# Computing the first four FFN column tiles during the initial weight load, and keeping w_down resident

## The chip, the cores and the metric

The kernel runs on one core of a Trainium2 chip. The metric is the device time of one execution in microseconds; before the change it is 2283.39 us, the median of 13 runs (2270.49 to 2290.09).

## What is computed

Two branches over the same x (2048 tokens of 1024, bf16) are mixed token by token with a sigmoid gate. Branch A walks over 64 segments of 32 tokens, strictly one after the other, since each hands eight memory rows to the next. Branch B is a gated feed-forward net (FFN) with 3584 inner columns, and needs nothing of branch A. Cut to what matters:

```
g = sigmoid((x * gate_w).sum(-1, keepdims=True))
for s in range(64):                              # branch A
    h = concat(mem, x[32*s : 32*s+32])           # 8 + 32 rows of 1024
    q, k, v = h @ Wq, h @ Wk, h @ Wv             # 32 heads of 128
    p = softmax(mask(q @ k.T / sqrt(128)))
    o = (p @ v) @ Wo
    mem, a[s] = o[:8], o[8:]
b = (gelu_tanh(x @ w_gate) * (x @ w_up)) @ w_down   # branch B
out = g * a + (1 - g) * b
```

## The kernel before

The kernel is one list of operations (`op`), each put on one of five engines: TensorE (pe), ScalarE (act), VectorE (dve), GpSimd (pool) and SyncE (sp, which only issues DMAs). Each engine works through its own part of the list in the order written. `_Prog` derives the waits from the byte ranges and PSUM banks that each operation reads and writes; for a PSUM bank it waits for the last operation of every other engine on that bank, reader or writer. An operation that waits holds up everything written behind it on its engine. A DMA named with a lane also waits for the previous DMA of that lane to have landed.

Three stages follow one another.

**The prologue** (lines 465 to 492). x comes in 16 tiles of 128 tokens through eight buffers `px`. `do_x(T)` transposes a tile on TensorE into PSUM bank 6 or 7 (line 426). ScalarE copies half of it into `xq` (L433), VectorE the other half (L434), and VectorE copies the last eight tokens of each segment into `xr` (L435). ScalarE's queue then issues the writes of both to the scratch tensors `xq_scr` (L437) and `xr_scr` (L440). For the gate, GpSimd multiplies the tile by gate_w into the single buffer `gp` (L442), and VectorE sums it into a column of `dl` (L444). So GpSimd's next product waits for VectorE's sum. Between these, SyncE's queue loads the attention weights in pieces of 512 KB into SBUF slots `sl` (L364).

Each of Wk, Wq, Wv and Wo has 16 pieces, 64 in all, for 52 slots. Twelve slots (`PAIRS`) are shared by two pieces each, so that they are loaded again in every segment: `spent` issues the next load when a piece has been used. `first` issues the first load of a slot. The buffers of the prologue lie in the 13 slots of Wo, so that these are first loaded within segment 0, at its second step (line 803).

**The attention** (lines 772 to 901). Every segment is a list of 64 products (`proj`; L678 for k, q and v, L690 for o) in the order k0 q0 v0 k1 q1 o0 v1 o1, where 0 and 1 are halves of the heads. Between them stand scores, softmax and the product with v. The last eight tokens of four segments at a time are projected as "fills" (L705). They are evacuated (L578), some are transposed (L590), and the results go to scratch through two buffers `stage` and GpSimd's queue (L751, lane `fq`; L746). Segment 0 does ten such fills itself (`fill0`).

**The FFN** (lines 948 to 1027). Tokens go in four blocks of 512 (`fb`). For each block, a loop over the 28 column tiles `j` does two groups of eight 128x512 matmuls, gate and up (L958), into one of two pairs of banks. The gelu follows in five operations: Square (ScalarE, L968), a VectorE product (L969), Tanh (ScalarE, L972), and two VectorE products (L973, L976), the last of which writes `GT[:, j]`. Then two passes over w_down (L1017, and L999 at the very end) make the output of the block, and `mix` combines it with branch A. w_gate and w_up stay in SBUF once loaded, in five chunks of `CH` = 2, 5, 7, 7, 7 column tiles. w_down streams through three 1 MB buffers `wd` (L549), 49 loads, and is loaded whole into `wl` for the last pass (L992). x comes back from `xq_scr` (L530). `early` lists the FFN loads that are issued within the last segment. `last_tail` finishes branch A after the seventh column tile of block 0 and then issues the rest of the first loads.

Of the kernel before, what the change touches and what calls it, by code (L numbers as in the profile page):

```python
# [195 lines left out]
def bass_gated_mix__memory_aug_recurrent_mem_tr__geglu_ffn__prompt_kernel(  # L196
# [19 lines left out]
    SEG = 32  # L216
# [14 lines left out]
    with ExitStack() as es:  # L231
# [14 lines left out]
        a_scr = nc.dram_tensor("a_scr", [NSEG, SEG, D], BF16)  # L246

# [74 lines left out]
        for m in "kqvo":  # L322
            for i in range(8):
                if i in PAIRS[m]:
                    hosts.append([(m, 0, i), (m, 1, i)])
                else:
                    hosts += [[(m, 0, i)], [(m, 1, i)]]
# [68 lines left out]
        cur[0] = slots[home["o", 0, 0]].off  # L396
        NPX = min(NT, 8)
# [4 lines left out]
        xq = [al(f"xq{i}", [128, 4, KC, SEG]) for i in range(2)]  # L402
        xr = [al(f"xr{i}", [128, KC, 4, NB]) for i in range(2)]
        hR1 = al("hR1", [128, KC, 32])
        dl = al("dl", [128, NT], FP32)
        assert cur[0] <= top
        memT = al("memT", [128, 64], at=oRc.off)
        hT = hTs[0]

# [9 lines left out]
        def do_x(T):  # L419
            t = px[T % NPX]  # L420
            b = 6 + T % 2
            x2 = T % 2

            def f(e):
                for kc in range(KC):
                    ins = e.transpose(PBV[b][:, kc * 128:(kc + 1) * 128], t[:, kc * 128:(kc + 1) * 128], ident[:, :])
                return ins
            op("pe", f, rd=[t.r(), ident.r()], wr=[BK(b)])
            pv = PBV[b].rearrange("p (k i c) -> p i k c", k=KC, i=4)
            h = (hR, hR1)[T] if T < 2 else None  # L430
            to = h[:, :, :].rearrange("p k (i c) -> p k i c", i=4) if h else xr[x2][:, :, :, :]
            to_r = h.r() if h else xr[x2].r()
            op("act", lambda e: e.activation(xq[x2][:, 0:2, :, :], pv[:, 0:2], ACTF.Copy), rd=[BK(b)], wr=[xq[x2].r(0, 512)])  # L433
            op("dve", lambda e: e.tensor_copy(xq[x2][:, 2:4, :, :], pv[:, 2:4]), rd=[BK(b)], wr=[xq[x2].r(512, 1024)])  # L434
            op("dve", lambda e: e.tensor_copy(to, PBV[b].rearrange("p (k i c) -> p k i c", k=KC, i=4)[:, :, :, NR:SEG]),  # L435
               rd=[BK(b)], wr=[to_r])
            op("act", lambda e: e.dma_start(xq_scr[T, :, :, :], xq[x2][:, :, :, :].rearrange("p i k c -> p i (k c)")),  # L437
               rd=[xq[x2].r()], wr=[("D", "xq", T)], lane=f"xw{x2}")
            if T > 0:
                op("act", lambda e: e.dma_start(xr_scr[T], to.rearrange("p k i c -> p (k i c)")),  # L440
                   rd=[to_r], wr=[("D", "xr", T)], lane=f"xv{x2}")
            op("pool", lambda e: e.tensor_tensor(out=gp[:, :], in0=t[:, :], in1=gwb[:, :], op=ALU.mult),  # L442
               rd=[t.r(), gwb.r()], wr=[gp.r()])
            op("dve", lambda e: e.tensor_reduce(dl[:, T:T + 1], gp[:, :], AX.X, ALU.add), rd=[gp.r()], wr=[dl.r(T, T + 1)])  # L444

# [23 lines left out]
        load_x(1)  # L469
        load_x(2)  # L470
        for n, p in enumerate(range(16)):
            first(at_step(p, 0))
            if n + 3 < NPX:
                load_x(n + 3)
        op("pe", tr_mem, rd=[pm.r(), ident.r()], wr=[BK(5)])
        op("dve", lambda e: e.tensor_copy(memT[:, :], PBV[5][:, 0:64]), rd=[BK(5)], wr=[memT.r()])
        for T in range(NT):
            do_x(T)
            load_x(T + NPX)
            if T == 0:  # L480
                load_h(0)
                op("dve", lambda e: e.tensor_copy(hT[:, :, NR:32], memT[:, :].rearrange("p (k c) -> p k c", k=KC)),
                   rd=[memT.r()], wr=[hT.r()])
        for p in range(16, 24):
            first(at_step(p, 0))
        for mr in (("k", 1), ("q", 1), ("v", 1)):
            for i in range(8):
                first((*mr, i))
# [3 lines left out]
        op("dve", lambda e: e.reciprocal(gal[:, :], dl[:, :]), rd=[dl.r()], wr=[gal.r()])  # L492


        cur[0] = res0
        FB = min(S, 512)
        NFB = S // FB
        TB = FB // 128
        NPS = (TB + 1) // 2
        xT = al("xT", [128, TB, 4, KC, SEG])  # L500
        WD = 4
        wd = [al(f"wd{i}", [128, WD, D]) for i in range(3)]
        GT = al("GT", [128, NJ, FB])
        CH = (2, 5, 7, 7, 7)
        assert sum(CH) == NJ
        jch = [(c, jj) for c, n in enumerate(CH) for jj in range(n)]
        wg, wu = [], []
        for c, n in enumerate(CH):
            wg.append(al(f"wg{c}", [128, KC, n * 128]))
            wu.append(al(f"wu{c}", [128, KC, n * 128]))  # L510
        assert cur[0] <= top
        free = [(low, res0), (cur[0], top)]
# [8 lines left out]
        tp = [al2(f"tp{t}", [128, FB], FP32) for t in range(2)]  # L521
        s1 = al2("s1", [128, FB], FP32)
        assert s1.off < res0
# [10 lines left out]
        def load_w(c):  # L534
            c0, c1 = sum(CH[:c]) * 128, sum(CH[:c + 1]) * 128
# [4 lines left out]
        NWD = NJ // WD  # L540
        nwd = [0]

        def load_wd():
            n = nwd[0]
            nwd[0] += 1
            if n >= (NFB * NPS - 1) * NWD:
                return
            c = n % NWD
            op("sp", lambda e: e.dma_start(wd[n % 3][:, :, :],  # L549
                                           B_w_down[c * WD * 128:(c + 1) * WD * 128, :].rearrange("(j p) f -> p j f", p=128)),  # L550
               wr=[wd[n % 3].r()], lane=f"wd{n % 3}")
# [22 lines left out]
        early = [lambda: load_xT(0), lambda: load_w(0), lambda: load_w(1), load_xo, lambda: load_w(2)]  # L574
# [197 lines left out]
        for s in range(NSEG):  # L772
# [24 lines left out]
            if s == 0:  # L797
# [5 lines left out]
                on("q", 0, 0, lambda: [first(("o", u, i)) for u in range(2) for i in range(8)])  # L803
# [102 lines left out]
        def last_tail():  # L906
# [8 lines left out]
            for n in range(3):  # L915
                load_wd()

        C_GELU = 0.7978845608028654
        SQ = 0.044715 ** 0.5
# [28 lines left out]
        for fb in range(NFB):  # L948
            HB, DN = ((0, 1, 2, 3), (4, 5, 6, 7)) if fb % 2 == 0 else ((4, 5, 6, 7), (0, 1, 2, 3))
            for j in range(NJ):  # L950
# [4 lines left out]
                for bk, w in ((bg, wg[c]), (bu, wu[c])):  # L955
                    def f(e, bk=bk, w=w, cc=cc):
                        for kc in range(KC):
                            ins = e.matmul(PB[bk][:, 0:FB], lhsT=w[:, kc, cc:cc + 128],  # L958
                                           rhs=xT[:, :, :, kc, :].rearrange("p t i c -> p (t i) c"),
                                           start=(kc == 0), stop=(kc == KC - 1))  # L960
                        return ins
                    pe_j = op("pe", f, rd=[w.r(), xT.r()], wr=[BK(bk)])
                while held:
                    put(held.pop(0), 0, D, after=[pe_j])
                hg, hu = PB[bg][:, 0:FB], PB[bu][:, 0:FB]
                t = tp[j % 2]
                gt = GT[:, j, :]
                op("act", lambda e, hg=hg: e.activation(s1[:, :], hg, ACTF.Square, scale=SQ), rd=[BK(bg)], wr=[s1.r()])  # L968
                op("dve", lambda e, hg=hg, t=t: e.scalar_tensor_tensor(out=t[:, :], in0=s1[:, :], scalar=1.0, in1=hg,  # L969
                                                                      op0=ALU.add, op1=ALU.mult),  # L970
                   rd=[BK(bg), s1.r()], wr=[t.r()])
                op("act", lambda e, t=t: e.activation(t[:, :], t[:, :], ACTF.Tanh, scale=C_GELU), rd=[t.r()], wr=[t.r()])  # L972
                op("dve", lambda e, hu=hu, t=t: e.scalar_tensor_tensor(out=t[:, :], in0=t[:, :], scalar=1.0, in1=hu,  # L973
# [90 lines left out]
```

## Time and profile before

| what | us |
|---|---|
| median of 13 runs | 2283.39 |
| lowest and highest run | 2270.49 and 2290.09 |
| the profiled execution's own time | 2290.09 |
| its span | 2288.2 |
| prologue: start to the first fill on TensorE | 0 to 72.7 |
| segment 0: from there to the first product of segment 1 | 72.7 to 141.3 |
| segments 1 to 62 | 141.3 to 1666.9 |
| last segment, up to the first FFN matmul | 1666.9 to 1694.3 |
| FFN | 1694.3 to 2288.2 |

The profile is of one execution, which was the slowest of the 13 runs. The span runs from the first to the last instruction; 1.9 us of the execution's own time lie around it. The stage bounds were read off the timeline: 72.7 is the start of the first instruction of line 705, 141.3 the start of segment 1's first instruction of line 678, and 1694.3 the first of line 958. "PE" is TensorE's matmuls, "PEld" its weight loads, which overlap them.

### The profile page before, as it was taken

How to read it: one execution, taken by the hardware profiler on the slowest of the kernel's cores; microseconds unless marked ns; L12 is line 12 of the kernel's file. 1: busy time of each engine (PE TensorE's matmuls, PEld its weight loads, DVE VectorE, ACT ScalarE, POOL GpSimd, SP SyncE). 2: the span in 40 equal slices, each digit the busy share in tenths (PEclk: the TensorE clock that was granted, in tenths of full speed). 3: DMA queues.
4: the chain of work that ended last, by engine and by line, in shares of the span. 5: the costliest groups of instructions: out<-in, count | busy, mean ns of one | idle time of the engine just before them, and what ended most of it. 6: DMA issues, size and time to landing. Idle time of an engine off the chain costs nothing.

```text
span 2288.2 us, 80087 instructions
## 1 busy us (share of the span) xinstructions
PE 2083.5 (91%) x36623; PEld 1104.9 (48%) x36642; DVE 913.7 (40%) x2166; ACT 604.8 (26%) x1280; POOL 616.3 (27%) x1137
## 2 busy tenths in 40 slices
PE   2589899999999899999899999998889999999999
PEld 1244545555555555555455554554444444444444
DVE  3234333433334334433334433334335346163462
ACT  1123232232223232232223223232223123031230
POOL 5232333243343333343243343333210000000000
PEclk6799999999999999999999999999999999999999
DMA  9968778888788788878888878888895440703622
GB/s 354 386 205 302 271 264 297 295 276 293 275 282 302 282 283 302 292 278 292 280 282 308 283 273 288 292 283 301 274 320 200 144 155 15 285 28 117 237 88 92
DMA packets 224369, 576.44 MB, mean 252 GB/s; under 512 B 30616, under 2 KB 43416, under 8 KB 224032
## 3 DMA queue, kind: packets, MB, share of 16 engines
q1 hardware_dynamic: 190400, 513.88, 62.6%
q0 software_dynamic: 29024, 52.01, 7.2%
q8 instruction: 287, 4.70, 0.8%
q10 hardware_dynamic: 4608, 5.44, 0.7%
q14 instruction: 50, 0.41, 0.0%
HBM read 539.71 MB, written 31.39 MB: 250 GB/s over the span
## 4 chain that ended last, share of the span: by engine, by line
PE 77%; DMA 12%; issue 5%; POOL 4%; DVE 1%; ACT 1%; SPq 0%; POOLq 0%; DVEq 0%; ACTq 0%
PE pb L678 25%; PE pb L958 17%; PE pb L690 8%; PE pb L1017 7%; PE pb L705 7%; PE pb L590 4%; DMA sl<-in_A_Wv_dram 4%; DMA sl<-in_A_Wo_dram 3%; PE pb L720 3%; DMA a_scr<-a_bf 2%; PE pb L611 2%; PE pb L605 1%; DMA xr_scr<-xr 1%; PE pb L999 1%; PE pb L644 1%
## 5 line engine op out<-in xcount | busy, mean ns | idle before, releaser
L678 PE MATMUL pb<-sl,hT 128*32 128x512 bf16 x12288 | 752.7, 383 | 28.6 <-issue 14.1
L678 PEld LDWEIGHTS pb<-sl,hT 128*32 128x32 bf16 x12288 | 335.4, 97 | 298.3 <-issue 28.0
L690 PE MATMUL pb<-sl,oT 128*32 128x256 bf16 x8192 | 280.8, 276 | 46.5 <-issue 40.1
L578 ACT ACTIVATE tok<-pb 128x512 bf16<-128x512 f32 x320 | 191.0, 597 | 425.5 <-PE pb L678 366.8
L663 POOL COPY oRc<-oT 128x128 bf16<-128x128 bf16 x128 | 97.5, 761 | 656.3 <-DVE oT L581 637.8
L690 PEld LDWEIGHTS pb<-sl,oT 128*32 128x32 bf16 x8192 | 208.8, 97 | 93.1 <-issue 45.3
L705 PE MATMUL pb<-sl,hR 128*32 128x512 bf16 x3072 | 229.7, 389 | 18.9 <-DVE xr L435 6.5
L958 PE MATMUL pb<-xT,wg 128*128 128x512 bf16 x896 | 213.4, 381 | 3.9 <-DMA wg<-in_B_w_gate_dram 3.9
L958 PE MATMUL pb<-xT,wu 128*128 128x512 bf16 x896 | 212.2, 380 | 0.0
L1017 PE MATMUL pb<-wd,GT 128*128 128x512 bf16 x766 | 168.6, 379 | 1.7 <-DMA wd<-in_B_w_down_dram 0.7
L581 DVE CAST oT<-pb 128x160 bf16<-128x160 f32 x256 | 71.2, 320 | 225.8 <-PE pb L654 225.5
L578 ACT ACTIVATE vA<-pb 128x512 bf16<-128x512 f32 x128 | 76.4, 597 | 278.5 <-PE pb L678 278.5
L968 ACT ACTIVATE s<-pb 128x512 f32<-128x512 f32 x112 | 66.9, 597 | 308.8 <-PE pb L958 308.8
L581 DVE COPY kT<-pb 128x512 bf16<-128x512 bf16 x128 | 51.9, 405 | 234.8 <-POOL kT L764 100.5
L958 PEld LDWEIGHTS pb<-xT,wg 128*128 128x128 bf16 x896 | 87.8, 98 | 110.7 <-issue 6.2
L590 PE MATMUL pb<-ident,tok 128*128 128x128 bf16 x1280 | 127.5, 222 | 14.8 <-DVE stg L581 5.3
L958 PEld LDWEIGHTS pb<-xT,wu 128*128 128x128 bf16 x896 | 87.9, 98 | 106.4 <-issue 1.1
L590 PEld LDWEIGHTS pb<-ident,tok 128*128 128x128 bf16 x1280 | 73.0, 98 | 125.7 <-ACT tok L578 93.9
L969 DVE SCALAR_TENSOR_TENSOR tp<-s,pb 128x512 f32<-128x512 f32 x112 | 76.9, 686 | 135.9 <-ACT s L968 135.5
L942 POOL DMA_DIRECT2D out_dram<-osb x14 | 7.6, 543 | 428.9 <-PE pb L958 267.1
L1017 PEld LDWEIGHTS pb<-wd,GT 128*128 128x128 bf16 x784 | 76.5, 98 | 93.8 <-DMA wd<-in_B_w_down_dram 2.1
L616 DVE TENSOR_REDUCE st<-pb 128x8 f32<-128x320 f32 x128 | 62.9, 492 | 147.3 <-PE pb L611 147.3
(80 smaller groups left out, 2055.1 us busy)
## 6 DMA issues: line engine op xcount, KB each, us to landing
sl<-in_A_Wv_dram SPq DMA_DIRECT2D x394, 512.0 KB, 8.9
sl<-in_A_Wo_dram SPq DMA_DIRECT2D x205, 512.0 KB, 5.9
sl<-in_A_Wk_dram SPq DMA_DIRECT2D x142, 512.0 KB, 5.6
wd<-in_B_w_down_dram SPq DMA_DIRECT2D x49, 1024.0 KB, 5.3
sl<-in_A_Wq_dram SPq DMA_DIRECT2D x79, 512.0 KB, 7.0
qk_scr<-stg POOLq DMA_DIRECT2D x64, 128.0 KB, 6.1
qkr<-qk_scr POOLq DMA_DIRECT2D x128, 64.0 KB, 2.2
wl<-in_B_w_down_dram SPq DMA_DIRECT2D x7, 1024.0 KB, 7.7
```

The costliest lines, as they stand in the source:

```text
L578: op("act", lambda e: e.activation(o, i, ACTF.Copy), rd=rd, wr=wr)
L581: op("dve", lambda e: e.tensor_copy(o, i), rd=rd, wr=wr)
L590: ins = e.transpose(PBV[TT][:, j * 128:(j + 1) * 128], tok[:, j * 128:(j + 1) * 128], ident[:, :])
L663: op("pool", lambda e: e.tensor_copy(oRc[:, u, :, :].rearrange("p c x -> p x c"), oT[:, :, :, 32:40].rearrange("p g j c -> p (g j) c")), r ...
L678: ins = e.matmul(PB[bk][32 * g:32 * g + 32, :], lhsT=h[:, i, :], rhs=w[:, g * 512:(g + 1) * 512], start=(p % 8 == 0), stop=(p % 8 == 7))
L690: ins = e.matmul(PB[XO][32 * g:32 * g + 32, 0:256], lhsT=oT[:, gp_, 2 * jj + hh, 0:32], rhs=w[:, c:c + 256], start=(r == 0 and p % 8 == 0 ...
L705: ins = e.matmul(PB[b][32 * g:32 * g + 32, :], lhsT=h[:, k[2], :], rhs=w[:, g * 512:(g + 1) * 512], start=(n == 0), stop=(n == 7))
L720: ins = e.matmul(PB[b][32 * g:32 * g + 32, 0:256], lhsT=t[:, :, 2 * i + hh], rhs=w[:, c:c + 256], start=(ends[0] and i == 0 and hh == 0), ...
L958: ins = e.matmul(PB[bk][:, 0:FB], lhsT=w[:, kc, cc:cc + 128], rhs=xT[:, :, :, kc, :].rearrange("p t i c -> p (t i) c"), start=(kc == 0), s ...
L968: op("act", lambda e, hg=hg: e.activation(s1[:, :], hg, ACTF.Square, scale=SQ), rd=[BK(bg)], wr=[s1.r()])
L969: op("dve", lambda e, hg=hg, t=t: e.scalar_tensor_tensor(out=t[:, :], in0=s1[:, :], scalar=1.0, in1=hg, op0=ALU.add, op1=ALU.mult), rd=[BK ...
L1017: ins = e.matmul(PB[bank[2 * k + hf]][:, :], lhsT=GT[:, j, tb * 128:(tb + 1) * 128], rhs=w[:, jj, hf * 512:(hf + 1) * 512], start=(j == 0) ...
```

## The change

Two things change. First, the gate and up products and the gelu of the first four of the 28 column tiles (`NJP` = 4) are done in the prologue, for all four token blocks (`pre_j`), and written to a new scratch tensor `g_scr`; the FFN reads them back into `GT` (`load_g`) and loops over the other 24 tiles. For this, x is transposed into two block-wide buffers `xTp`, all by ScalarE. The writes of x to scratch are one DMA a block; there are four `px` buffers instead of eight; and the prologue's buffers take 15 slots, those of Wo and two of Wv, which are loaded after it. The attention loads are issued four ahead and then two per `pre_j` (`more`). Second, w_down lies in SBUF whole through the FFN (`wd`, seven tiles of 1 MB, loaded once).

```diff
+        NJP = 4
+        NJR = NJ - NJP
+        g_scr = nc.dram_tensor("g_scr", [NFB, 128, NJP * FB], BF16)
...
         for m in "kqvo":
...
+            hosts += [[(m, 0, i), (m, 1, i)] for i in PAIRS[m]]
+            for r in range(2):
+                hosts += [[(m, r, i)] for i in range(8) if i not in PAIRS[m]]
+        spare = len(hosts) - sum(h[0][0] == "o" or h[0][:2] == ("v", 1) for h in hosts)
...
-        cur[0] = slots[home["o", 0, 0]].off
-        NPX = min(NT, 8)
+        cur[0] = slots[spare].off
+        NPX = min(NT, 4)
+        xTp = [al(f"xTp{i}", [128, TB, 4, KC, SEG]) for i in range(2)]
+        wgp = al("wgp", [128, KC, NJP * 128])
+        wup = al("wup", [128, KC, NJP * 128])
+        gpre = [al(f"gpre{i}", [128, NJP, FB]) for i in range(2)]
...
+        def gelu(hg, hu, bg, bu, n, gt, gt_r):
...
+        def up(w, x, bk, cc):
+            def f(e):
+                for kc in range(KC):
+                    ins = e.matmul(PB[bk][:, 0:FB], lhsT=w[:, kc, cc:cc + 128],
+                                   rhs=x[:, :, :, kc, :].rearrange("p t i c -> p (t i) c"), start=(kc == 0), stop=(kc == KC - 1))
+                return ins
+            return op("pe", f, rd=[w.r(), x.r()], wr=[BK(bk)])
+
+        def pre_j(fb, j):
+            bg, bu = 2 * (j % 2), 2 * (j % 2) + 1
+            for bk, w in ((bg, wgp), (bu, wup)):
+                up(w, xTp[fb % 2], bk, 128 * j)
+            g = gpre[fb % 2]
+            gelu(PB[bg][:, 0:FB], PB[bu][:, 0:FB], bg, bu, j, g[:, j, :], g.r(j * FB, (j + 1) * FB))
+            if j == NJP - 1:
+                op("act", lambda e: e.dma_start(g_scr[fb], g[:, :, :].rearrange("p j c -> p (j c)")), rd=[g.r()],
+                   wr=[("D", "g", fb)], lane=f"gw{fb % 2}")
+
+        def load_g(fb):
+            op("sp", lambda e: e.dma_start(GT[:, 0:NJP, :].rearrange("p j c -> p (j c)"), g_scr[fb]), rd=[("D", "g", fb)],
+               wr=[GT.r(0, NJP * FB)], lane="gl")
...
-            op("act", lambda e: e.activation(xq[x2][:, 0:2, :, :], pv[:, 0:2], ACTF.Copy), rd=[BK(b)], wr=[xq[x2].r(0, 512)])
-            op("dve", lambda e: e.tensor_copy(xq[x2][:, 2:4, :, :], pv[:, 2:4]), rd=[BK(b)], wr=[xq[x2].r(512, 1024)])
...
+            op("act", lambda e: e.activation(x[:, tb, 0:2, :, :], pv[:, 0:2], ACTF.Copy), rd=[BK(b)], wr=[x.r(tb * n, tb * n + n // 2)])
+            op("act", lambda e: e.activation(x[:, tb, 2:4, :, :], pv[:, 2:4], ACTF.Copy), rd=[BK(b)], wr=[x.r(tb * n + n // 2, tb * n + n)])
+            op("dve", lambda e: e.tensor_copy(xr[:, tb, :, :, :], PBV[b].rearrange("p (k i c) -> p k i c", k=KC, i=4)[:, :, :, NR:SEG]),
+               rd=[BK(b)], wr=[xr.r(256 * tb, 256 * tb + 256)])
...
+            if tb == TB - 1:
+                op("act", lambda e: e.dma_start(xq_scr[TB * fb:TB * fb + TB].rearrange("t p i c -> p t (i c)"),
...
+                op("act", lambda e: e.dma_start(xr_scr[TB * fb:TB * fb + TB].rearrange("t p c -> p t c"),
...
-        for n, p in enumerate(range(16)):
-            first(at_step(p, 0))
-            if n + 3 < NPX:
-                load_x(n + 3)
+        for h in range(2):
+            for w, W, nme in ((wgp, B_w_gate, "gp"), (wup, B_w_up, "up")):
+                c0, c1 = h * NJP * 64, (h + 1) * NJP * 64
+                op("sp", lambda e, w=w, W=W, c0=c0, c1=c1: e.dma_start(w[:, :, c0:c1], W[:, c0:c1].rearrange("(kc p) c -> p kc c", p=128)),
+                   wr=[w.r()], lane=f"{nme}{h}")
...
+        more(4)
...
-        for T in range(NT):
+        for T in range(TB):
             do_x(T)
             load_x(T + NPX)
             if T == 0:
-                load_h(0)
...
+                op("dve", lambda e: e.tensor_copy(hT[:, :, 0:NR], xTp[0][:, 0, 0, :, 0:NR]),
+                   rd=[xTp[0].r(0, KC * SEG)], wr=[hT.r()])
...
+        for fb in range(NFB):
+            for j in range(NJP):
+                pre_j(fb, j)
+                T = TB * (fb + 1) + j
+                if T < NT:
+                    do_x(T)
+                    load_x(T + NPX)
+                more(2)
+        more(99)
...
+        for u in range(2):
+            for m in "vo":
+                for i in range(8):
+                    if home[m, u, i] >= spare:
+                        first((m, u, i))
...
-        CH = (2, 5, 7, 7, 7)
+        CH = (2, 5, 5, 6, 6)
...
+        wd = [al(f"wd{i}", [128, WD, D]) for i in range(NWD)]
...
-        early = [lambda: load_xT(0), lambda: load_w(0), lambda: load_w(1), load_xo, lambda: load_w(2)]
+        early = [lambda: load_xT(0), lambda: load_w(0), lambda: load_w(1), lambda: load_g(0), load_xo, lambda: load_w(2)]
...
-                on("q", 0, 0, lambda: [first(("o", u, i)) for u in range(2) for i in range(8)])
...
             load_w(4)
-            for n in range(3):
-                load_wd()
+            for c in range(NWD):
+                load_wd(c)
...
-            for j in range(NJ):
+            for j in range(NJR):
...
+                if j == 0 and fb > 0:
+                    load_g(fb)
...
-                    w = wd[((fb * NPS + ps) * NWD + c) % 3]
+                    w = wd[c]
...
-                    load_wd()
```

The new `gelu` holds the five operations of lines 968 to 978 as they were, and `up` the eight matmuls of lines 956 to 962.

## The prediction

> **What bounds the kernel now.** I read the page's slices first, then the stages cut into stretches, then the chain of waits. The slices (matmul tenths, granted clock, DMA share):
>
> ```profile
> PE   2589899999999899999899999998889999999999
> PEclk6799999999999999999999999999999999999999
> DMA  9968778888788788878888878888895440703622
> ```
>
> TensorE is full except in the first two of 40 slices, where the DMA engines are. Cut at the stage bounds (columns: matmul, weight load, VectorE, ScalarE, GpSimd busy, clock, DMA share, GB/s):
>
> ```profile
> 0.00:72.70 72.70, 16.75 (x140) 12.71 (x141) 28.46 (x50) 10.84 (x17) 37.72 (x36) 0.59 0.97 366
> 72.70:141.30 68.60, 48.27 (x800) 21.13 (x804) 13.44 (x35) 12.36 (x26) 17.57 (x32) 0.84 0.74 269
> 141.30:1666.90 1525.60, 1413.33 (x32428) 791.11 (x32432) 589.09 (x1657) 436.75 (x997) 536.26 (x1026) 0.99 0.81 286
> 1799.00:2288.20 489.20, 482.89 (x2249) 221.49 (x2266) 217.45 (x320) 103.30 (x169) 14.04 (x26) 1.00 0.38 136
> ```
>
> The reader is to see where TensorE time is worth something: the prologue leaves it idle for 56 of 72.7 us, the FFN for almost nothing. The chain (start, length, what) shows what paces the start:
>
> ```profile
> 43.07 2.13 POOL gp L442
> ...
> 47.20 9.38 DMA xr_scr<-xr
> ...
> 104.71 14.07 DMA sl<-in_A_Wv_dram
> ...
> 1847.30 96.69 PE pb L958 x448
> ...
> 1982.01 7.55 DMA wd<-in_B_w_down_dram
> ```
>
> The gp product and its sum alternate, then scratch writes of x gate the next tile. In segment 0 the Wv reload waits behind the 13 Wo loads that SyncE issued from 82.7 on. A whole FFN loop is TensorE alone. The last line looks like 7.55 us lost to w_down, but the timeline of TensorE says otherwise:
>
> ```profile
> 1974.70 14.19 PE L1017 MATMUL pb<-wd,GT 128*128 128x512 bf16 x63
> 1989.61 3.63 PE L1017 MATMUL pb<-wd,GT 128*128 128x512 bf16 x16 [0.72 <-DMA wd<-in_B_w_down_dram]
> ```
>
> It worked until 1988.89 and idled 0.72 us; the rest of the chain's step lay beside work.
>
> **What the Trainium skill says.** "TensorE: Matmul & The Clock Gate", Part 1, says that the clock is half until about 3.4 us of sustained activity, and half again after an idle window of that length. The trace agrees: clock 0.50 from 20 to 72.7, and in the FFN 0.50 from 1694.3 to 1698 after 3.9 us of idling, then 0.98. "DMA: Bandwidth & Descriptors", Issuing engines are not separate DMA queues, says that DMAs from all queues share 16 engines. It agrees: the 256 KB writes of x, on ScalarE's queue, land after 6.1 us (median) beside the weight stream, 2.0 at best. "ScalarE: Activation LUTs", What ACT_TABLE_LOAD costs, prices a change of function set; here the one before Tanh took 1.28 us.
>
> **The change part by part.**
>
> *FFN, removed.* Four tiles x two products x eight matmuls x four blocks = 256 matmuls. The loop took 96.69 us for 448, so 0.2158 each: 55.2 us, all on TensorE's path. Residence of w_down removes 49 MB of loads; what they cost TensorE is the idle before L1017, 0.7 us in matmuls and up to 2.8 with weight loads: I take 1.0. Sum **56.2**; ends 55 and 58.
>
> *FFN, added.* Four reads of 0.5 MB into GT. For blocks 1 to 3 each is issued at the loop's start and used 24 x 3.45 = 83 us later: nothing. Without that cover it would be some 6 us each (a 256 KB xT load lands in 6.0). The first stands behind xT and the first two chunks, so the 3.9 us wait for wg stays. The third chunk is due five tiles (17 us) after branch A's tail instead of seven (24 us). The last five tiles of it are 6.3 MB, and their slots are not those of the Wo copies any more, so they come no later. The seven w_down loads are due 24 tiles on. I count nothing.
>
> *Prologue, added.* The moved work meets a chain there. A step is pre_j plus one x tile. TensorE needs 16 x 0.2158 = 3.45, and about 0.5 for the transposes at full clock (1.03 at half): 3.97. VectorE, in its own order, needs three gelu products with Tanh between them, 2.80 from start to end as in the FFN (0.69 each, 0.63 Tanh, hand-overs), then the xr copy 0.28 and the sum 1.22: **4.35**. So VectorE paces the steps. The half copy of x that it gives up (0.42) goes to ScalarE.
> Start: the first four tiles keep the alternation of gp (2.12 + 1.22 + 0.1 = 3.45), from 8.0 on: the fourth sum ends at 8.0 + 3 x 3.45 + 1.2 = 19.5. TensorE could start at some 13; gate/up parts, x and gate_w, 3.4 MB at 412 GB/s, are there by 11.
> Block 0: three steps 13.1, the last gelu 2.8, a table load 1.28. Then ScalarE's queue, which holds the write of g until that gelu is done, issues it (0.4); behind it wait the last tile's two copies (1.25), and TensorE's next block needs those. 19.5 + 18.8 = 38.3.
> Blocks 1 and 2: at such a boundary TensorE stands still 3 us and more, and may be cold after it. The first step then ends (xr copied and summed) at 6.9 if nothing interferes; at 10.4 with half clock, or if xr, whose write is queued behind a 1 MB write of x and gates its buffer's reuse, lands at 9. Then two steps 8.7, a gelu 2.8, 1.65 as above: 13.15. So 20.1 to 23.6 a block; I take 22.5.
> Block 3 has no x: 4 x 3.45 plus up to 3.4 of half clock: 16. **Prologue end 38.3 + 45 + 16 = 99.3**, against 72.7. SyncE's queue carries the loads past it: each x load waits for the tile four before it, but the last x load is out by about block 2, and 17 of the 37 slots then go freely: 8.9 MB, 22 us, done at 82. It is not the DMA that sets this end.
>
> *Segment 0, moved.* The 15 late slots (7.9 MB, some 20 us) are issued at the prologue's end, ahead of everything, one of them after the last write of g. The scratch writes of the fills keep their pace (4.88, 7.90, 7.06 in the chain). But the Wv reload, issued some 27 us in, now finds the queue empty and lands at 27 + 3.1 MB/0.4 + 2 = 37 instead of 46.1. Saved 9; the Exp table comes back (1.3), the first fill is warm (1.7 less): 68.6 becomes **60**; ends 56 and 68.6.
> Segment 1 starts at 99.3 + 60 = 159.3 instead of 141.3: **+18.0**.
>
> *Segments 1 to 63*: the same pieces in the same order, at other addresses. Nothing.
>
> Sum: -56.2 + 18.0 = **-38.2**. The profiled execution took 2290.1 (span 2288.2 and 1.9 around it), 6.7 above the median of the runs; it becomes 2251.9, and the median 2283.4 becomes **2245**.
>
> **The rivals.** *Free prologue*: the new work hides entirely and the DMA sets its end: 33 MB (37 slots 19.4, x 4.2, gate/up 2.1, writes 7.3) at 412 GB/s plus 2 us: 83, segment 0 in 58: 141. Nothing added, **2227**. For it: 56 us of idle TensorE, DMA at 0.97. Against: gp and its sum paced the tiles already, and VectorE gets 33 us of gelu (48 x 0.69) on top.
> *Deep boundaries*: each boundary costs a full landing (9.4, the longest in the chain) and a cold start one after the other: blocks of 28, prologue end 38 + 56 + 18 = 112, segment 0 in 63: 175, +34, **2261**. For it: landings of 7 to 9 us beside the weight stream. Against: the stream is thinner then, two slots a step.
> *Half clock throughout*, the one that ends slower: the gaps keep TensorE at 0.50 as they do now. A step is 6.9 + 1.03 = 7.95, a block with boundary 34, and the last 27.6: 13 + 3 x 34 + 27.6 = 143; segment 0 keeps 68.6: 211, +70, less 56.2: +14, **2297**. It decides from a prologue end of 72.7 + 56.2 = 129 on. For it: 0.50 from 20 to 72.7. Against: there TensorE worked 13.5 of 52.7 us; at 72.7, once busy, it was at full clock within 3.6 us (the first fill 3.63, the next 1.9).
> *It doesn't do what it says*: the FFN gives back the tiles because another engine binds it. VectorE has 2.07 and ScalarE 1.23 a tile against TensorE's 3.45, so hardly. **2283**.
>
> **How the numbers follow.** Mine 0.56, own range 2232 to 2257 (prologue end 94 to 105, segment 0 in 56 to 64); free prologue 0.20; deep boundaries 0.15; half clock 0.05; no effect 0.04. From the lower third of the free prologue's chance to most of the deep boundaries': 2224 to 2266. A measurement of this kernel can tell about 0.3% from no change (7 us): faster 0.91, same 0.04, slower 0.05.
>
> **What would show it.** The first fill starts at 94 to 105, in free prologue at 83, in half clock beyond 129. The steps within a block are about 4.35 apart, with VectorE nearly always busy, and the gap at block boundaries is filled on TensorE by a wait for ScalarE's copies. TensorE's clock lies at 0.8 or more from 20 to 99. Segment 1 starts 56 to 64 after the first fill, and no Wv step stands in segment 0's chain like the 14.07. An FFN loop takes 24 x 3.453 = 82.9, and the idle before the w_down products is gone. I am wrong if segments 1 to 63 change by more than 3 us, if the prologue ends beyond 112, or if the FFN loses less than 55.

## The result, and the profile after

The changed kernel takes 2263.53 us, the median of 11 runs (2257.07 to 2276.03); the kernel before, run beside it, 2282.05, the median of 48 runs (2270.49 to 2293.66). The ratio is **0.9927, 95% interval 0.9909 to 0.9945**: 0.0073 x 2282 = 17 us are gained, where 38 were forecast. The profiled execution took 2268.98 us, its span is 2267.2, against a span of 2288.2 before.

The slices of the page (matmul tenths, granted clock, DMA share), beside those of before:

```profile
PE   6579999999899999989999999999888999999999
PEclk8899999999999999999999999999999999999999
DMA  8767788888788778878878878878879600100000
```

TensorE now works in the first two slices, at a high clock, and w_down's stream is gone from the last eight. But the DMA digit of the first two slices fell from 9 and 9 to 8 and 7: the weight stream of the prologue has holes. Cut at the same stage bounds as before (columns as in the prediction):

```profile
0.00:120.70 120.70, 78.98 (x393) 36.98 (x393) 53.39 (x81) 38.42 (x66) 37.87 (x37) 0.86 0.77 272
120.70:182.80 62.10, 45.21 (x801) 20.25 (x801) 13.62 (x36) 12.61 (x27) 17.54 (x31) 0.89 0.73 264
182.80:1703.00 1520.20, 1410.18 (x32402) 788.76 (x32406) 588.58 (x1655) 436.63 (x995) 534.76 (x1023) 0.99 0.82 287
1821.00:2267.20 446.20, 441.02 (x2057) 202.86 (x2074) 192.84 (x284) 88.49 (x145) 14.04 (x26) 1.00 0.08 28
```

The bounds are the same instructions as before: the first fill, the first product of segment 1, the last segment, the first w_down product.

| stage | before | after | change | forecast |
|---|---|---|---|---|
| prologue | 72.7 | 120.7 | +48.0 | +26.6 |
| segment 0 | 68.6 | 62.1 | -6.5 | -8.6 |
| segment 1 to the first FFN matmul | 1553.1 | 1547.9 | -5.2 | 0 |
| FFN | 593.9 | 536.6 | -57.3 | -56.2 |
| span | 2288.2 | 2267.2 | -21.0 | -38.2 |

Segment 0 and the FFN come out near the forecast; segments 1 to 63 are taken up at the end. The miss is in the first row: the prologue ends 21.4 us later than the 99.3 of the prediction. What stands in it, from the chain of waits (start, length, what):

```profile
3.55 8.18 DMA wup<-in_B_w_up_dram
16.02 9.76 DMA px<-in_A_x_dram
...
43.95 14.81 DMA xr_scr<-xr
...
72.97 18.31 DMA xr_scr<-xr
105.09 13.96 PE pb L440 x56
...
1869.21 82.88 PE pb L440 x384
```

Two writes of 256 KB, of `xr`, take 14.81 and 18.31 us from issue to landing, 33 of the 121 us. The chain's length is not yet the loss, since other work can lie beside it; the timelines give that (start, length, instruction, in brackets the idle time ahead of it and what ended it). Two lines of VectorE's:

```profile
58.86 0.29 DVE L482 COPY xr<-pb 128x256 bf16<-128x256 bf16 x1 [8.46 <-DMA xr_scr<-xr]
91.37 0.29 DVE L482 COPY xr<-pb 128x256 bf16<-128x256 bf16 x1 [13.42 <-DMA xr_scr<-xr]
```

and two of TensorE's:

```profile
19.41 2.69 PE L440 MATMUL pb<-xTp,wup 128*128 128x512 bf16 x8 [2.01 <-DMA wup<-in_B_w_up_dram]
43.57 2.95 PE L440 MATMUL pb<-xTp,wgp 128*128 128x512 bf16 x8 [3.06 <-ACT xTp L481]
```

VectorE, which paces the steps, stands still for 8.46 and 13.42 us: the copy into `xr` for a new block must wait until the block before has been written out of that same buffer. Behind the copy stand the gate sum and all gelu products, so TensorE, ScalarE and GpSimd stop one after the other, and so does SyncE, whose next load of x waits until TensorE has transposed and GpSimd has multiplied the tile in `px`, with the attention loads queued behind it. TensorE's lines show two smaller things: the first up product starts at 19.41, and a block's first product waits 3.06 us for ScalarE's copies. SyncE's own waits in the first 130 us (in total, times, longest) show the holes in the weight stream (the first two lines: both are waits ahead of a load of x, and L143 is the line in which every engine waits) and a reason for the late up product:

```profile
SPq L143 <- PE pb L476: 26.1, 7, 7.6
SPq L466 <- POOL gp L484: 16.8, 7, 9.2
...
SPq L526 <- DMA wgp<-in_B_w_gate_dram: 5.7, 1, 5.7
...
SPq L526 <- DMA wup<-in_B_w_up_dram: 1.1, 1, 1.1
```

The parts of gate and up come in two halves each, and the second half of a tile is not issued before the first has landed.

Why does the write take so long? The DMA queues while the second of them is in flight (packets, MB, share of the 16 engines; q1 is SyncE's queue, q10 ScalarE's):

```profile
q1 hardware_dynamic: 1420, 5.13, 74.1%
q10 hardware_dynamic: 1200, 1.84, 26.7%
```

and in the trace of before, while such a write of one tile was in flight (47.2 to 56.6):

```profile
q1 hardware_dynamic: 834, 3.03, 82.1%
q10 hardware_dynamic: 590, 0.68, 20.1%
```

In 18.31 us ScalarE's queue moved 1200 packets, 65.5 a microsecond; before, 590 in 9.38 us, 62.9. In bytes the two rates are far apart, 0.100 and 0.072 MB/us. Ahead of `xr` stand the 0.5 MB write of the four gelu tiles (`g`), in 128 pieces of 4 KB, and the 1 MB write of x, in 512 pieces of 2 KB; then come its own 512 pieces of 512 bytes. The profile counts a piece as a packet: these are 1152 of the 1200, and the rest carries next to no bytes. "DMA: Bandwidth & Descriptors", Queues, rings and completion order, of the Trainium skill says that each DMA engine takes turns between the queues it has work for, a packet at a time. A packet of that page gathers several descriptors, while the profile counts pieces, so the counts here, 1420 against 1200, lie near to such turns but don't show them; during the first of the two writes they were 721 against 1200. The experiments test what the landing depends on.

### The profile page after: what moved, and what is told of

Read it like the earlier page. It is cut to its first block, busy times and chain, and to the rows that moved or that the text cites. A ratio compares the mean times of both kernels' runs of the same rounds, so it can differ in the third digit from the quotient of the medians.

```text
span 2267.2 us, 80030 instructions
## 1 busy us (share of the span) xinstructions
PE 2084.4 (92%) x36623; PEld 1101.9 (49%) x36642; DVE 905.8 (40%) x2151; ACT 612.1 (27%) x1296; POOL 616.6 (27%) x1138
## 3 DMA queue, kind: packets, MB, share of 16 engines
q1 hardware_dynamic: 169264, 464.59, 57.3%
## 4 chain that ended last, share of the span: by engine, by line
PE 78%; DMA 11%; issue 4%; POOL 3%; DVE 3%; ACT 1%; SPq 0%; ACTq 0%; DVEq 0%; POOLq 0%
PE pb L734 26%; PE pb L440 16%; PE pb L746 9%; PE pb L1047 7%; PE pb L761 7%; PE pb L646 4%; PE pb L776 3%; DMA sl<-in_A_Wo_dram 3%; DMA a_scr<-a_bf 2%; DMA sl<-in_A_Wv_dram 2%; PE pb L667 2%; DMA xr_scr<-xr 1%; PE pb L661 1%; PE pb L700 1%; PE pb L1029 1%
## 5 line engine op out<-in xcount | busy, mean ns | idle before, releaser
L440 PE MATMUL pb<-xT,wg 128*128 128x512 bf16 x768 | 183.0, 381 | 4.2 <-DMA wg<-in_B_w_gate_dram 4.2
L440 PE MATMUL pb<-xT,wu 128*128 128x512 bf16 x768 | 181.4, 379 | 0.0
L672 DVE TENSOR_REDUCE st<-pb 128x8 f32<-128x320 f32 x128 | 62.9, 492 | 148.0 <-PE pb L667 148.0
L440 PEld LDWEIGHTS pb<-xT,wg 128*128 128x128 bf16 x768 | 75.3, 98 | 96.0 <-issue 6.5
L440 PEld LDWEIGHTS pb<-xT,wu 128*128 128x128 bf16 x768 | 75.2, 98 | 90.9 <-issue 0.5
```

## The experiments

The theory: the wait of VectorE for the landing of `xr`, because of the single buffer, is the loss; its size comes from the number of packets ahead of it in ScalarE's queue. The rivals differ from run to run: the boundary's other parts, a late start, the volume of the weight stream, the pace of VectorE.

| kernel | median us (runs) | ratio to before, 95% | starts of blocks 0 to 3 | prologue end | segment 1 |
|---|---|---|---|---|---|
| changed kernel | 2263.53 (11) | 0.9927 (0.9909 to 0.9945) | 14.1, 43.6, 72.6, 105.1 | 120.7 | 182.8 |
| e1_xr2 | 2245.16 (4) | 0.9852 (0.9821 to 0.9883) | 13.9, 43.7, 64.4, 85.3 | 100.9 | 163.9 |
| e2_few_packets | 2255.05 (6) | 0.9902 (0.9873 to 0.9931) | 13.9, 42.7, 67.3, 92.2 | 109.0 | 169.8 |
| e3_one_load | 2261.36 (6) | 0.9921 (0.9893 to 0.9949) | 12.3, 38.8, 65.3, 98.1 | 112.0 | 174.6 |
| e4_no_products | 2234.71 (5) | 0.9819 (0.9788 to 0.9850) | - | 76.0 | 153.3 |
| e5_xr_first | 2253.20 (6) | 0.9880 (0.9851 to 0.9909) | 14.0, 42.0, 63.8, 89.5 | 105.1 | 168.2 |
| e6_streamed | 2262.90 (6) | 0.9939 (0.9918 to 0.9960) | 14.0, 44.8, 72.8, 105.0 | 118.9 | 181.0 |
| e7_together | 2231.27 (4) | 0.9794 (0.9771 to 0.9817) | 12.5, 34.6, 53.3, 70.5 | 84.4 | 150.7 |
| e8_tile_first | 2232.97 (5) | 0.9789 (0.9764 to 0.9814) | 15.7, 34.4, 52.2, 70.0 | 84.8 | 148.3 |
| e9_wo_later | 2240.86 (5) | 0.9820 (0.9800 to 0.9841) | 12.4, 34.4, 52.0, 69.7 | 83.6 | 155.9 |
| e10_wo_last | 2236.75 (6) | 0.9821 (0.9789 to 0.9854) | 12.4, 34.5, 52.1, 69.5 | 83.4 | 149.0 |

Each ratio is to runs of the kernel before that were made beside the experiment, so gains below are taken from the ratios and not from the medians. Stage times are of the one profiled execution. A block starts with its first gate product on TensorE. The starts are read off the timelines and settle questions of a few microseconds that the ratios alone can't; e6, which leaves the prologue as it is, shows how far two profiles of the same prologue lie apart (118.9 and 120.7).

**e1_xr2: a second `xr` buffer.**

```diff
+        xrB = al("xrB", [128, TB, KC, 4, NB])
-        xr = al("xr", [128, TB, KC, 4, NB])
+        xrA = al("xr", [128, TB, KC, 4, NB])
...
+            xr = (xrA, xrB)[fb % 2]
```

> A second xr buffer, one for each parity of the block, so that a block's first xr copy no longer waits for the landing of the block before's write. Theory A (the landing of that write gates VectorE's queue, which waited 8.46 and 13.42 us for it, and with it the gelu behind it): the starts of the blocks on TensorE, now 29.0 and 32.5 us apart, come to 20 to 23 us apart, the prologue ends at 100 to 105 instead of 120.7, and the time falls by 15 to 20 us, to about 2246. Rival V (VectorE's own work of 4.35 us a step, or a cold TensorE clock, paces the blocks): they stay at 27 or more, the prologue ends beyond 115, and the time falls by less than 5.

The windows of the prologue and segment 0:

```profile
0.00:100.86 100.86, 75.61 (x392) 35.87 (x392) 53.40 (x81) 38.85 (x66) 37.91 (x37) 0.92 0.92 325
100.86:163.90 63.04, 45.00 (x797) 20.15 (x796) 13.58 (x36) 12.61 (x27) 17.56 (x31) 0.89 0.72 261
```

The prologue ends 19.8 us earlier with the same work (53.40 us on VectorE against 53.39), and the DMA share rises from 0.77 to 0.92. The writes still land late, up to 19.5 us after issue, but nobody waits for them. The blocks are 20.7 and 20.9 long where they were 29.0 and 32.5. The gain reaches the time: 0.9852 against 0.9927 of before. A single buffer of 2 KB a partition is the cause of most of the miss.

**e2_few_packets: the same bytes in fewer pieces.** The scratch tensors are laid out so that each partition's share of a block is one piece, and the readers are changed to match:

```diff
-        xq_scr = nc.dram_tensor("xq_scr", [NT, 128, 4, KC * SEG], BF16)
+        xq_scr = nc.dram_tensor("xq_scr", [NT // 4, 128, 4, 4, KC * SEG], BF16)
-        xr_scr = nc.dram_tensor("xr_scr", [NG, 128, KC * 32], BF16)
+        xr_scr = nc.dram_tensor("xr_scr", [NG // 4, 128, 4, KC * 32], BF16)
```

> The same bytes written, but the scratch tensors of x and xr are laid out so that a partition's part of a block is one piece (8 KB and 2 KB) instead of four (2 KB and 512 B). Theory P (a write on ScalarE's queue takes as long as its packets, each of which takes its turn with one packet of the weight stream): xr, which lands after 14.8 and 18.3 us, lands after 6 to 10, the prologue ends at 103 to 110, and the time falls by 10 to 17 us. Rival B (bytes decide: 1.75 MB share the engines with the weights): the landings stay within 3 us of what they were and the time within 4.

The queues while the second `xr` write is in flight:

```profile
q1 hardware_dynamic: 721, 2.38, 57.5%
q10 hardware_dynamic: 432, 1.84, 41.5%
```

and VectorE's timeline at the two copies that wait:

```profile
53.57 0.29 DVE L482 COPY xr<-pb 128x256 bf16<-128x256 bf16 x1 [4.04 <-DMA xr_scr<-xr]
78.44 0.29 DVE L482 COPY xr<-pb 128x256 bf16<-128x256 bf16 x1 [4.10 <-DMA xr_scr<-xr]
```

The same 1.84 MB go out in 432 packets instead of 1200; ScalarE's queue gets 41.5% of the DMA time instead of 26.7%, and `xr` lands after 10.72 us instead of 18.31, the first write after 10.43 instead of 14.81. So bytes alone don't decide. That is the direction that taking turns packet by packet demands, but not its size: SyncE's queue moved 721 packets in that time, not some 432, and 432 at the 65.5 a microsecond of above would have taken 6.6 us. Larger pieces were served more slowly, piece for piece. The landings are a little over the 6 to 10 expected, and the wait is not gone. The prologue ends at 109.0, as expected, but the time falls by some 6 us, less than the 10 to 17 expected, and the intervals overlap.

**e3_one_load: gate and up parts in one load each.** In the changed kernel each half is declared as writing the whole tile (`wr=[w.r()]`), hence SyncE's waits of 5.7 and 1.1 us shown above.

```diff
-        for h in range(2):
+        for h in range(1):
-                c0, c1 = h * NJP * 64, (h + 1) * NJP * 64
+                c0, c1 = 0, NJP * 128
```

> The first gate and up weights come as one 1 MB load each instead of two halves. Theory S (each second half waits for the first half to land, since both are put down as writing the whole tile, and SyncE's queue with the x tiles and attention weights waits behind it): the up weights land at 12 to 14 instead of 19.4, the first block ends some 5 us earlier (next block's start at 38 to 40 instead of 43.6), and the time falls by 4 to 6 us if the later waits don't swallow it. Rival: the start is paced by the tile sums on VectorE (to 20.2 now) and nothing moves by more than 2 us.

Block 1 starts at 38.8 instead of 43.6, as expected. Blocks 2 and 3 keep the lead and add to it (65.3 against 72.6, 98.1 against 105.1), although VectorE still waits 5.86 and 12.16 us for `xr` in blocks 1 and 2. Segment 1 comes 8 us earlier in the profile; the ratio, 0.9921 (0.9893 to 0.9949), can't be told from the changed kernel's. So the late start is shown in the profile, and its worth in the time is not resolved.

**e4_no_products: the prologue without the added products.**

```diff
-            for bk, w in ((bg, wgp), (bu, wup)):
-                up(w, xTp[fb % 2], bk, 128 * j)
-            gelu(PB[bg][:, 0:FB], PB[bu][:, 0:FB], bg, bu, j, g[:, j, :], g.r(j * FB, (j + 1) * FB))
...
+        for g in gpre:
+            op("dve", lambda e, g=g: e.memset(g[:, :, :], 0.0), wr=[g.r()])
```

> Leaves out the gate and up products and the gelu of the first four column tiles altogether (zeros are written to scratch in their place); everything else of the change stays. Theory A: the prologue is then the x tiles, two attention loads at a time and the wait for the xr write, and ends at 75 to 85; so most of the 48 us that the prologue grew by are the moved work and the waits that it meets. Rival O (the new order of the loads, four x buffers and two loads a step, is itself what costs): it still ends beyond 95. The time falls against the changed kernel by 30 to 45 us under A, by less than 25 under O.

The prologue ends at 76.0, within what was expected and 3.3 us after that of before; so the new order of the loads costs little, and the moved work with its waits is nearly all of the growth. But segment 0 then takes 77 us instead of 62, so that segment 1 comes only 29.5 us earlier, not 45. VectorE still waits for `xr` in two blocks, 7.94 and 7.49 us, although no product and no gelu is there. Two steps of the chain follow:

```profile
75.94 12.06 DMA xr_scr<-xr
...
108.16 12.86 DMA sl<-in_A_Wk_dram
```

This was a half miss. Part of what is taken out of the prologue is given back in segment 0, where the last write of `xr` and the loads are awaited. The time goes to 0.9819 against 0.9927, about 25 us less, at the border of the two sides; it doesn't decide between them, and the prologue's end does.

**e5_xr_first: the `xr` write ahead of the x write.** The order of the two issues on ScalarE's queue is exchanged, nothing else:

```diff
+                op("act", lambda e: e.dma_start(xr_scr[TB * fb:TB * fb + TB].rearrange("t p c -> p t c"),
                 op("act", lambda e: e.dma_start(xq_scr[TB * fb:TB * fb + TB].rearrange("t p i c -> p t (i c)"),
...
-                op("act", lambda e: e.dma_start(xr_scr[TB * fb:TB * fb + TB].rearrange("t p c -> p t c"),
```

> Only the order on ScalarE's queue is changed: the 256 KB write of xr is issued ahead of the 1 MB write of x of the same block. Theory P (the queue's packets are served in order, taking turns with the weight stream): of the 1200 packets that stood before the end of the xr write, the 512 of x now stand behind it, so it lands after 7 to 11 us instead of 14.8 and 18.3; the prologue ends at 103 to 112 instead of 120.7 and the time falls by 10 to 16 us. Rival (the write of xr is slow by itself, by its 512-byte pieces): it still lands after 13 us or more and the time moves by less than 5.

From the chain:

```profile
42.30 7.65 DMA xr_scr<-xr
...
64.07 11.55 DMA xr_scr<-xr
```

The landing falls from 14.81 and 18.31 to 7.65 and 11.55, with the same pieces of 512 bytes. So those are not slow by themselves; what stands ahead in the same queue makes the difference. In the second window ScalarE's queue moved 744 packets, 64.4 a microsecond, the rate of the two windows above again. In the first it moved 1065 in 7.65 us, 139 a microsecond, while SyncE's queue moved 347: the rate depends on what the other queue has to do. VectorE still waits 1.21 and 5.11 us; the write of `g` is ahead of it in the queue as before. The prologue ends at 105.1 and the time falls by about 11 us by the ratios, both as expected.

**e6_streamed: w_down streamed as before the change.** The other part of the change undone: three `wd` buffers, 49 loads and the last pass's seven.

```diff
-        wd = [al(f"wd{i}", [128, WD, D]) for i in range(NWD)]
+        wd = [al(f"wd{i}", [128, WD, D]) for i in range(3)]
...
-                    w = wd[c]
+                    w = wd[((fb * NPS + ps) * NWD + c) % 3]
...
+                    load_wd()
```

> Undoes one part: w_down streams through three buffers again, 49 loads and 7 for the last pass, as in the kernel before; the moved tiles stay. The prediction's own term: TensorE idles some 1 us in all before the w_down products, so the time rises by 0 to 3 us against the changed kernel, which is within the noise. Rival (the 7.55 us step of the chain was a real loss, or the streams disturb the x and scratch reads beside them): it rises by 6 us or more.

The chain of this kernel again holds a wait for w_down, as before's did, which says nothing on its own:

```profile
1847.15 6.92 DMA wd<-in_B_w_down_dram
```

The timeline of TensorE over the same time:

```profile
1839.84 21.53 PE L1060 MATMUL pb<-wd,GT 128*128 128x512 bf16 x95
```

TensorE runs through from 1839.84 to 1861.37. Over all w_down products the idle time ahead of them is 2.2 us, where it was 2.8 before the change and is none with w_down resident. The FFN takes 537.8 us against 536.6, but the ten profiles with w_down resident lie between 536.6 and 537.7 themselves, and the time ratio, 0.9939 against 0.9927, is no clear difference. So the 1 us that was counted for residence fits and isn't resolved, and the 6 us of the rival don't show in the FFN.

**e7_together: the causes removed together.** The edits of e1, e2 and e3; the first four attention loads one after each of the first four x tiles instead of ahead of x tile 4; the write of `g` issued behind the last tile's copies and writes.

```diff
-        more(4)
...
             load_x(T + NPX)
+            more(1)
...
-            if j == NJP - 1:
+        def put_g(fb):
...
+                if j == NJP - 1:
+                    put_g(fb)
```

> Four edits of the prologue together: two xr buffers, one-piece scratch layouts, one load each for the first gate and up weights, the first four attention loads issued one after each x tile; and the write of the four gelu tiles is issued behind the copies of the last x tile on ScalarE's queue. If VectorE's step of 4.35 us is what remains, the blocks start 17.5 to 19 us apart, the prologue ends at 90 to 95, and the time is some 24 us below the changed kernel's; if the weight stream (33 MB) then sets the pace, segment 1 starts no earlier than in the kernel without the products (153), and the time is 18 to 22 below.

```profile
0.00:84.39 84.39, 68.88 (x394) 34.57 (x394) 52.77 (x81) 37.85 (x66) 37.96 (x37) 0.98 0.98 363
84.39:150.70 66.31, 45.97 (x797) 20.37 (x796) 13.58 (x36) 12.60 (x27) 17.50 (x31) 0.85 0.75 281
```

The prologue ends at 84.4, earlier than expected. It holds the added work, and the DMA engines are as full as in the prologue of before (0.98 against 0.97). The time is **2231.27, 0.9794 (0.9771 to 0.9817)** of before, about 30 us under the changed kernel by the ratios, more than either side expected. But segment 0 is at 66.3, and a step of the chain in it is the Wk reload that e4 had.

**e8_tile_first: another order within the step.** e1, e2, e3 and the spread loads, with the transposes and copies of an x tile ahead of the step's products, so that ScalarE's copies at the boundary are not behind the gelu:

```diff
             for j in range(NJP):
-                pre_j(fb, j)
                 T = TB * (fb + 1) + j
...
+                pre_j(fb, j)
```

> As in the run before it, but instead of moving the write of the gelu tiles, each x tile is transposed and copied ahead of its step's products instead of after them, so that a block's products never wait for the last tile's copies. If boundaries still cost TensorE 3 us each, the prologue ends 5 to 8 us earlier than with the four edits together, at 85 to 88; if VectorE's steps alone pace it, it ends within 3 us of it. The time is within 5 us of it either way, since segment 0 then waits for its weights.

Prologue end 84.8, time 2232.97: within 2 us of e7, so the boundary's wait for copies no longer bounds. The DMA share of 0.97 suggests that the stream of loads and writes does. The chain says otherwise: from 13 us to the prologue's end it holds no DMA, in e7 neither. It repeats VectorE's steps, with ScalarE's part between them (one step; the copy of `xr` ends it):

```profile
65.94 1.21 DVE dl L491
67.15 0.60 DVE tp L430
67.78 0.64 ACT tp L432
68.44 0.70 DVE tp L433
69.16 0.69 DVE gpre L435
...
```

Such a step takes 4.03 us, the one at a block's boundary 5.7, and three of the first and one of the second make the 17.8 us by which the blocks lie apart. So VectorE's steps pace this prologue, as the expectation said for an end within 3 us of e7, and full DMA engines stand beside it.

**e9_wo_later and e10_wo_last: the order of the late loads.** To see whether segment 0 waits for the order of SyncE's loads or for their volume, two versions of e7 put the 15 slots that are loaded last elsewhere. In e9 all of them come with the first Wv product:

```diff
-        for u in range(2):
+        def late():
...
+                on("v", 0, 0, late)
```

> All edits of e7_together, and the 15 late slots (13 Wo, 2 Wv) are issued at the first Wv product of segment 0 instead of at the prologue's end, so that the reloads of Wk and Wq stand ahead of them in SyncE's queue. Theory A' (in e4, e7 and e8 segment 1 starts at 148 to 153 because the Wk reload stands behind the 15 late slots: 105.9 to 117.9 in the chain of e7, 7.6 us of idle TensorE in front of it): prologue end stays at 84 to 86, no Wk load in segment 0's chain, segment 1 starts 5 to 9 us earlier, at 142 to 146, time 2222 to 2227. Rival V (it is the volume: 24 loads, 12.6 MB at 0.4 MB/us, 31 us from the prologue's end on, in whatever order): the wait moves to the Wo or Wv products, segment 1 stays at 149 to 152, time 2229 to 2233. Rival S (the scratch round trip of the fills, qk_scr and v_scr and hR, paces segment 0 anyway): segment 1 at 148 to 150 with those steps longer in the chain.

In e10 the two Wv slots stay, and the 13 of Wo come behind all reloads:

```diff
+        late("v")
...
+                on("k", 1, 0, lambda: late("o"))
```

> All edits of e7_together; the 2 late Wv slots are issued at the prologue's end as before, the 13 late Wo slots only behind the reloads of Wk, Wq and Wv, ahead of the first product of the second half of Wk. In e9 the Wo loads stood ahead of the Wv reloads instead, and TensorE idled 17.1 us for those. Theory order (SyncE's order of these loads decides segment 0): 11 loads, 5.5 MB, some 14 us at 0.4 MB/us, are all that stands before the fills of the second half; the Wo loads, 6.8 MB, follow and land by about 130, where the first o products stand: segment 1 at 141 to 146, prologue end unchanged at 84 to 86, time 2222 to 2227. Rival volume: the same bytes are needed by the o products anyway, so that these wait instead: segment 1 at 148 to 152, time 2229 to 2233.

TensorE's longest wait in segment 0 of e9:

```profile
127.64 0.62 PE L768 MATMUL pb<-sl,hR 128*32 128x512 bf16 x4 [17.12 <-DMA sl<-in_A_Wv_dram]
```

and of e10:

```profile
134.61 1.05 PE L769 MATMUL pb<-sl,hR 128*32 128x512 bf16 x8 [10.65 <-DMA hR<-xr_scr]
```

Both expectations of a gain fail. In e9 the Wk wait of e7 (7.55 us) is gone and one of 17.12 for Wv, now behind the Wo loads, stands in its place: segment 1 at 155.9, later than any of the three sides expected. In e10 no reload costs more than 1.7 us, and TensorE then stands 10.65 us for the read of `hR`, which is issued only when the fills' results have gone through scratch (the chain shows 6.03 for a qk write, 4.79 for a v write and 4.95 for the read of hR). In e7 those last two took 3.26 and 2.09. Segment 1 starts at 149.0, against 150.7 in e7, and the time doesn't fall. That is the place which the volume rival gave, but not its mechanism, since it expected the o products to wait; it is the rival of e9 in which the scratch round trip paces segment 0. No run here takes both chains away at once, so what segment 0 would cost without either is open.

## Why the prediction was right in sign and wrong in size

**The FFN, removed: right.** A loop was to take 24 x 3.453 = 82.9; it takes 82.88. The sum was -56.2; the stage gave -57.3. The 1.0 for residence in it is too small to be resolved (e6).

**Segments 1 to 63: nothing shown.** The profile has -5.2, beyond the 3 us that were to make the prediction wrong. But the eleven profiles of changed kernels put this stage at 1540.9 to 1549.7 with the same work in it, and the single profile of before has 1553.1. Nor does the lead of the changed kernel grow over the segments: counted from segment 1, by the first reduction of the scores in a segment, it is 7.5 us at segment 21, 0.1 at 37 and 2.4 at 61. The timed runs give -17, the sum of the other stages -15.8 (48.0 - 6.5 - 57.3). A change here is neither needed nor excluded within a few microseconds.

**Segment 0: nearly right.** 62.1 against 60, inside the ends given, with no Wv step in its chain.

**VectorE paces the steps: right.** Within a block the copies of `xr` are 4.03 us apart (58.86, 62.89, 66.92), against 4.35; TensorE's own part of such a step, from one gate product to the next, is 3.90. The boundary's wait for ScalarE's copies is there, 3.06 us. Block 3 takes 15.6 against 16.

**Half clock throughout: refuted.** The mean clock of the prologue is 0.86, against 0.59 before. That it is so because the work is dense enough is the prediction's reason; it fits (TensorE works 79.0 of 120.7 us instead of 16.75 of 72.7), but no run here tests it.

**Blocks 1 and 2, the step that failed.** The prediction had a block of 20.1 to 23.6, with a first step that ends at 6.9 undisturbed and "at 10.4 with half clock, or if xr, whose write is queued behind a 1 MB write of x and gates its buffer's reuse, lands at 9", and took 22.5. Mechanism and place were right. The size was not: `xr` landed after 14.81 and 18.31, not 9, and the blocks took 29.0 and 32.5, not 22.5 each: **16.5 us of the 21.4** by which the prologue ended late. With the measured landings the prediction's own sum comes within 1 us: the first steps end 16.7 and 20.2 us after the block's start instead of 10.4, and with its 13.15 for the rest that makes 29.9 and 33.4. Without the wait (e1) the blocks are 20.7 and 20.9, near the 20.1 of the prediction's lower end. The 9 is close to the longest landing in the chain of before, 9.38 us. That write was of 64 KB behind writes of one or two tiles; the changed kernel queues four times the bytes of x and `xr` at a time, in pieces of the same size, and `g` besides. A better estimate could be had from the trace of before: 62.9 packets a microsecond in ScalarE's queue, and some 1152 pieces to go, 18.3 us. This was worked out afterwards, and it is not exact: the second write took 18.31 us for 1200 packets, and the first 14.81 for as many, 81 a microsecond, beside a thinner weight stream.

**The start, the second miss: +5.3 us.** Block 1 started at 43.6 instead of 38.3. The prediction had "gate/up parts, x and gate_w, 3.4 MB at 412 GB/s, are there by 11", a sum of bytes. But SyncE waited 5.7 us between the halves, and the up part was used at 19.41; x tile 4, issued at 16.02 behind four attention loads, was 9.76 us on its way. e3 takes the first part away and brings block 1 to 38.8.

The four blocks add up: +5.3, +6.5, +10.0 and -0.4 make 21.4. **Deep boundaries** was the nearest rival: a landing at each boundary, though in full and with a cold start. It gave 112 for the prologue's end and 2261 for the time; 120.7 and 2263.5 were measured. The landing was longer than its 9.4, and the cold start, a clock at half, came at some of the starts and in part: after 3.06 and 3.85 us of idle TensorE the first gate product took 2.95 and 3.04 us (mean clock 0.62 and 0.60), after 2.97 us it took 1.90 (clock 1.00). That its time is so near is in part luck, since the prologue was 8.7 us off. **Free prologue** came near in its number only in e7, once the waits were gone: an end at 84.4 against its 83. Its mechanism didn't: VectorE, not the DMA, sets that end, and segment 0 takes 66.3 and not 58.

## What to carry to other kernels

When a change merges small writes into large ones, price the landing by what stands ahead of it in its own queue, and by the rate at which the trace shows that queue being served with pieces of that size beside a stream like that, not by the longest landing seen so far; and ask who reuses the source buffer. A buffer that is written out by a DMA and refilled by the engine that paces everything needs a second copy: here 2 KB a partition were worth about 17 us. A wait that is taken away shows its worth only after the next chain has been found: in segment 0 here, Wk, Wv and the scratch round trip took each other's place. And a DMA share near 1 says that the engines are busy, not that anybody waits for them: look whether the chain holds a DMA.

## What the runs showed of the hardware that was not expected

Beside a full weight stream ScalarE's queue was served at 62.9, 65.5 and 64.4 packets a microsecond in three windows with quite different bytes (0.68, 1.84 and 0.93 MB); with larger pieces (e2) at 40, for 0.172 MB/us instead of 0.100. Beside a thinner stream it was served faster: 81 and 139 in the two windows with 721 and 347 packets of SyncE's.

Issuing such a write can hold up ScalarE itself. At the starts of blocks 1 and 2 the third of three writes issued within some 2 us took long to issue, whichever it was: `xr` 2.19 and 1.46 us in the changed kernel and 1.30 and 1.06 in e2, x 1.24 and 1.62 in e5, `g` 1.68 and 0.66 in e7. The first two took 0.33 to 0.42. In e8, where `g` follows some 4 us later, it took 0.33 like the others.
